# Re-timing of batch 2's value sums, batch 7's attention and the middle weights' conversion

## The chip, the cores and the metric

The kernel runs on one core of one Trainium2 chip. The metric is device time in microseconds (us) of one execution. The engines are PE (TensorE: matmuls; PEld its weight loads), DVE (VectorE), ACT (ScalarE), POOL (GpSimd) and SP (SyncE, which here only issues DMAs). Each takes its instructions strictly in the order in which they stand in its own stream; semaphores hold an instruction until what it reads or overwrites is ready.

## The reference

Eight batches (0 to 7) go through three layers. The first is attention with pooled keys and values (576 queries, keys and values averaged over groups of 8 to 72, 8 heads of 64); the second ("moe") turns its output `x` into `x*cos(theta)` and `x*sin(theta)`, mixes over tokens with two 576x576 weights and then over channels with `w_ch`; the third ("moe2") is two two-layer perceptrons.

```python
k_p = k.reshape(B, H, Sp, 8, D).mean(axis=3); v_p = ...        # Sp = 72
scores = scale * q @ k_p^T;  scores -= max
attn = exp(scores);  attn /= sum + 1e-9;  x = attn @ v_p
theta = x @ w_theta
zr, zi = x * cos(theta), x * sin(theta)
u = x + w_tok_r @ zr + w_tok_i @ zi
x = u + relu(u @ w_ch)
h = relu(x^T @ w_tok1) @ w_tok2;  u = x + h^T
out = u + relu(u @ w_ch1) @ w_ch2
```

## The kernel before

**Values in two parts.** Most products are made in a 32-bit form that keeps fewer bits than fp32, so an operand is split into a high and a low part (`Xh`/`Xl`, `vbh`/`vbl`, the two halves of `Z`), and each product is three matmuls. The weights arrive as 64-bit numbers; a *conversion* of one piece (`cq_step`, L251 to L278) makes it fp32 with operations on its two 32-bit words and then splits it (high part on ACT L302, low part on POOL or DVE L304). In its mode 2 the first operation, which drops the sign, is a bitwise AND on DVE (L257); in mode 1 it is an Abs on ACT (L231).

**A batch.** It has scores for four pairs of heads (`emit_sc`: `x<-bdk,q` on PE, maximum L547 and subtraction L548 on DVE, exponential L553 on ACT), the normalisation (`emit_norm`: sum L560, reciprocal L564 on DVE, scaling of `e` L565 and two small copies into `pl` L570 on POOL), transposes of the attention weights on PE (`emit_pt`, four of `e` and one of `pl`, L181), attention times values (`emit_av`: `x<-pt,vbh`, `x<-pt,vbl`, `x<-t,vlh`), theta in column groups of two token halves (`emit_theta`: `t<-wth`; cosine and sine L735 to L748, whose last two ACT operations, L741 and L742, use another activation table than the exponential), and `Z` (`emit_z`: product L766 on DVE, high part L780 on ACT, low part L781 on POOL). `x` below also names the PSUM banks through which scores, transposes of `R` and `x` for L766 go; a bank is free for the next user when the DVE operation that reads it is done.

**Token mixing.** For each of 8 output tiles (j, th) of a batch 27 matmuls `m<-wtk,Z` (24) and `m<-wtk,zt` (3) are added up in PSUM, 256 or 320 columns wide, and DVE adds the sum to `R` (L819, and L2273 for batch 0), after which `R` is stored (`scr_u`, SP).

**Key and value sums.** DVE sums groups of 8: `prep_k` (L406, from `kr`), `prep_v` (L416 from `vr`, and after a copy on ACT the low part L423 from the one buffer `sums`), `prep_vl` (L438 from `vlr`). `vr` has one buffer, so that the second half of a batch's values is loaded when the first has been summed.

**What sets the order.** Batch 0, and the attention and part of theta and Z of batch 1, are ordered by a planner (`first_batches`, L1777 to L2280). After it `issue_after(behind)` puts the first loads and sums for batch 2 behind all that it planned. For batches 1 to 7 `interleave` puts the 72 mixing steps of batch b (3 matmuls each) in order and *side steps* among them: attention and half of theta of batch b+1, loads and sums of batch b+2. A side step is issued at a due time of the table `P` in us of matmul work since the start of the batch. The framework then reorders each engine's stream by what it holds ready, so an instruction can end up well ahead of the place where it is issued. The middle weights (`w_ch`, `w_tok1`, `w_tok2`; 15 pieces of DVE work and more for the tails) are converted in batch 7 by `begin` and 19 `cq_step`s; they are used from 510 us on. The third layer follows from there and is not touched.

Of the kernel before, what the change touches and what calls it, by code (L numbers as in the profile page):

```python
# [19 lines left out]
P = {  # L20
    "lo": 0.24,
    "sc": (6.25, 8.41, 12.28, 13.41),
    "norm": 3.97,
    "pt": (22.02, 23.22, 25.71, 29.04, 30.75),
    "av": (26.38, 27.79, 31.91, 31.99),
    "th1": (0, 3.17),
    "z1": (5.39, 9.51),
    "th0": (36.38, 36.77, 37.89),
# [14 lines left out]
    "f_prep": (0.93, 4.0, 10.52, 8.07),  # L43
    "f_ws": (5.53, 0),
    "pl": (2, 2, 0, 0),
    "l_cq": (1.26, 1.0),
    "l_u": (11.67, 22.91, 4.84),
    "l_th1": (3.39, 3.6),
    "l_z1": (3.91, 8.29),
    "l_n": (0.0, 4.89, 2.84),  # L50
    "a_n": (2.91,),
    "a_cq": (1, 3, 5, 7),
    "a_th": (0,),
    "a_tr": 4,
    "md": (1.7, 2.0),
    "mo": 1,
}
F64_FLOOR = 2.0 ** -15
# [14 lines left out]
def tile_attn_moe(  # L73
# [20 lines left out]
    B = qT.shape[0]  # L94
# [26 lines left out]
    def later(dt, fn, *tags):  # L121
        dseq[0] += 1
        heapq.heappush(dq, (clk[0] + dt, dseq[0], fn, tags))
        tick()

    def flush():
        while dq:
            run_one()

    def st(tag, shape, dt, name=None):  # L130
        need(tag)
        return sb.tile(shape, dt, tag=tag, name=name or tag)
# [258 lines left out]
    def load_v(b, g):  # L391
        t = st("vr", [128, 2, 512], F32)
        nc.sync.dma_start(out=t, in_=vm[b, 2 * g:2 * g + 2].rearrange("g p t -> p g t"))
        vr_t[b, g] = t

    def load_vl(b):
        t = [st(x, [128, 512], F32, "vlr") for x in ("vlr", "n2")]
        for g in range(2):
            for r in range(3):
                nc.sync.dma_start(out=t[g][32 * r:32 * r + 32], in_=vl[b, 32 * g:32 * g + 32])  # L400
        vlr_t[b] = t
# [11 lines left out]
    def prep_v(b, g):  # L413
        vr = vr_t.pop((b, g))
        vs = st("sums", [128, 2, 64], F32)
        nc.vector.tensor_reduce(  # L416
            out=vs, in_=vr.rearrange("p g (d o) -> p g d o", o=8), axis=AX.X, op=ALU.add
        )

        def fin():  # L420
            for e in range(2):
                pr = slice(64 * e, 64 * e + 64)
                nc.vector.tensor_sub(  # L423
                    out=vlo["b"][pr, 2 * g:2 * g + 2, pr], in0=vs[pr],
                    in1=vbh[pr, 2 * g:2 * g + 2, pr].bitcast(F32),
                )

        for e in range(2):
            pr = slice(64 * e, 64 * e + 64)
            nc.scalar.copy(out=vbh[pr, 2 * g:2 * g + 2, pr], in_=vs[pr])  # L430
        later(1.0, fin, "sums", "vbl")

    def prep_vl(b):
        vr = vlr_t.pop(b)
        vs = st("vls", [128, 2, 64], F32)
        vh = st("vlsh", [128, 2, 64], F32R)
        for g in range(2):
            nc.vector.tensor_reduce(  # L438
                out=vs[0:96, g], in_=vr[g][0:96].rearrange("p (d o) -> p d o", o=8), axis=AX.X, op=ALU.add
            )  # L440
        nc.scalar.copy(out=vh[0:96], in_=vs[0:96])
        nc.gpsimd.tensor_sub(out=vh[32:64], in0=vs[32:64], in1=vh[32:64].bitcast(F32))
        m4 = mask[0:96, 0:4].unsqueeze(2)
        for g in range(2):
            nc.gpsimd.tensor_tensor(
                out=vlt[0:96, 2 * g:2 * g + 2].rearrange("p a e d -> p (a e) d"),
                in0=m4.to_broadcast([96, 4, 64]),
                in1=vh[0:96, g].bitcast(F32).unsqueeze(1).to_broadcast([96, 4, 64]),
                op=ALU.mult,
            )  # L450
# [1871 lines left out]
    def side_next(b):  # L2322
        n = b + 1
        s = []
        f = "f_" if b == 0 else ""
        for p in range(4):
            s.append((P[f + "sc"][p], lambda p=p: emit_sc(n, p)))
            s.append((P[f + "sc"][p] + P[f + "norm"], lambda p=p: emit_norm(n, p)))
        for p, t in zip((0, 1, 4, 2, 3), P[f + "pt"]):
            s.append((t, lambda p=p: emit_pt(n, p)))  # L2330
        for j, t in enumerate(P[f + "av"]):
            for th in range(2):
                s.append((t + 0.6 * th, lambda j=j, th=th: emit_av(n, j, th)))
        for g, t0, t1, lo in zip((2, 0, 1), P[f + "th0"], P[f + "z0"], (nc.gpsimd,) * 3):
            s.append((t0, lambda g=g: emit_theta(n, 0, g)))
            s.append((t1, lambda g=g, lo=lo: emit_z(n, 0, g, lo)))
        return s
# [12 lines left out]
    if True:  # L2350
        behind = first_batches()
        with ExitStack() as s:
            for i in behind:
                s.enter_context(tc.issue_after(i))
            if B > 2:
                load_v(2, 0)
                load_vl(2)
                prep_v(2, 0)
                load_v(2, 1)
                prep_v(2, 1)  # L2360
                prep_vl(2)
            flush()
        for b in range(1, B):
            last = b == B - 1
            side = []
            f = "l_" if last else "f_" if b == 0 else ""
            for g, a, z, lo in zip((0, 1), P[f + "th1"], P[f + "z1"], (nc.gpsimd,) * 2):
                side.append((a, lambda g=g: emit_theta(b, 1, g)))
                side.append((z, lambda g=g, lo=lo: emit_z(b, 1, g, lo)))
            if not last:  # L2370
                side += side_next(b)
            if b + 2 < B:
                side += side_load(b + 2)
            if last:
                def begin():
                    zt = st(f"zt{(b + 1) % 2}", [128, CV, 2], U32, "late0")
                    vs = [st(x, [128, 256, 2], U32, f"late_{x}") for x in ("vbh", "vbl", "vlh", "vll")]
                    vr = st("vr", [128, 3, CV], F32, "late1")
                    n = [int(x + 0.5) for x in P["l_n"]]
                    cq_use((["stg0", "stg1", "bdk"] + ([zt] + vs)[0:n[0]]),  # L2380
                           (["cvt0", "vlr"] + [vr[:, i] for i in range(3)])[0:1 + n[1]])
                    lo_m[0] = max(2, n[2])
                    cq_mode[0] = min(2, int(P["md"][0] + 0.5))
                    add_wch()
                    add_tok1()
                    add_tok2()
                    cq_load()
                side.append((0.0, begin))
                for i in range(19):
                    side.append((P["l_cq"][0] + P["l_cq"][1] * i, cq_step))  # L2390
                side.append((P["l_u"][0], lambda: load_u(0)))
                for j in range(4):
                    side.append((P["l_u"][1] + P["l_u"][2] * j, lambda j=j: split_u(0, j)))
            interleave(mix_steps(b), side)
        flush()
        cq_step(20)
        wq[:] = weight_steps(0, 256, (W_TAGS[0:4], W_TAGS[4:6], W_TAGS[6:8], W_TAGS[8:13]), (0,) * 6)
        wstep(2)

        def ch(b):  # L2400
            order = [(j, th) for j in range(4) for th in range(2)]
            if b in P["a_th"]:
                order = [(j, th) for th in range(2) for j in range(4)]
            for i, (j, th) in enumerate(order):
                emit_ch(b, j, th)
                if b == 0 and P["a_tr"] == i:
                    emit_tr(0, 0)
                    emit_tr(0, 1)
                if i % 2 == 0:
                    wstep()  # L2410

        if B > 1:
            load_u(1)
        ch(0)
        if B > 1:
            for j in range(4):
                split_u(1, j)
        for c in range(2 if P["a_tr"] < 8 else 0, 5):
            emit_tr(0, c)
        for b in range(B):  # L2420
            if b + 2 < B:
                load_u(b + 2)
            for f in range(2):
                emit_tok1(b, f)
            if b + 1 < B:
                ch(b + 1)
            for j in range(4):
                for th in range(2):
                    emit_tok2(b, j, th)
                    if th == 0 and j % 2 == 0:  # L2430
                        wstep()
                    if j == 1 and th == 0 and b + 1 < B:
                        for c in range(5):
                            emit_tr(b + 1, c)
                if b + 2 < B:
                    split_u(b + 2, j)
        wstep(1000)
        flush()
        channel_mix()
# [62 lines left out]
```

## Time and profile before

| what | value |
|---|---|
| three runs | 1274.97, 1275.24, 1278.01 us, median 1275.24 |
| profiled execution, span | 1275.0 us |
| mean granted TensorE clock | 0.993 |
| PE busy | 1248.5 us, 98% |
| DVE, ACT, POOL busy | 953.2, 656.4, 302.7 us |
| PE idle longest in the part that the change touches | 2.06, 0.95, 1.63, 2.99 us |

The profile is of one execution, and its own time is its span of 1275.0 us. Times below count from the start of the span. The mixing of batch 1 begins at 121.8 us, that of batch 6 at 409.5, that of batch 7 a little before 470, and `w_ch` at 510.4. A row of a timeline gives start, duration, engine, line, operation, output <- inputs, shapes and count; in square brackets stand the idle time before it and what ended it. Rows of one kind are merged and may overlap the next by some 0.2 us, so work is measured from start to start.

### The profile page before, as it was taken

Reading aid. Unit: us, or ns where it says so; the run is one execution under the profiler, and the core shown is the slowest. Engines: PE = TensorE matmul, PEld = TensorE weight load, DVE = VectorE, ACT = ScalarE, POOL = GpSimd, SP = SyncE. Lnnn points to the kernel's source line nnn. Section 1 sums busy time; section 2 is a strip of 40 time slices with the busy share of each in tenths; the row PEclk is TensorE's granted clock in tenths of the full one; section 3 lists DMA queues with packets and bytes.
Section 4 is the critical chain, followed back from the end, with each engine's and each line's share of the span. In section 5 each row is a group of like instructions: output and inputs, shape, how many; then the busy total and the mean of one; then the engine's idle time right before and its main releaser. Section 6 shows DMA issues by size and latency. Waiting matters only on the chain.

```text
span 1275.0 us, 22259 instructions
## 1 busy us (share of the span) xinstructions
PE 1248.5 (98%) x8132; PEld 1205.9 (95%) x8132; DVE 953.2 (75%) x1739; ACT 656.4 (51%) x1264; POOL 302.7 (24%) x301
## 2 busy tenths in 40 slices
PE   8999999999999989999999999999999999999998
PEld 5789999999999989899999999999999899999998
DVE  7995868586675993867775689986644598988894
ACT  4856566656756663334422256665554445444442
POOL 1382424334242441211110022320000032213122
PEclk9999999999999999999999999999999999999999
DMA  9523433232221132666782488984448966546621
GB/s 337 157 79 103 141 96 112 71 112 72 94 87 36 45 99 88 212 211 237 260 292 75 157 287 277 299 279 155 139 146 293 369 217 203 183 139 215 204 88 63
DMA packets 122126, 214.50 MB, mean 168 GB/s; under 512 B 11744, under 2 KB 68576, under 8 KB 122016
## 3 DMA queue, kind: packets, MB, share of 16 engines
q1 hardware_dynamic: 122016, 213.08, 50.4%
q8 instruction: 64, 1.05, 0.3%
q14 instruction: 46, 0.38, 0.1%
HBM read 134.39 MB, written 78.64 MB: 167 GB/s over the span
## 4 chain that ended last, share of the span: by engine, by line
PE 76%; DVE 11%; DMA 7%; ACT 2%; issue 2%; SPq 1%; POOL 0%; DVEq 0%; ACTq 0%; POOLq 0%
PE m L167 28%; PE x L167 26%; PE t L167 19%; PE x L181 3%; DMA ws<-w_ch 1%; DMA early<-w_tok 1%; DMA scr_x<-u 1%; DMA early<-w_theta 1%; DMA scr_w<-wo 1%; DMA k<-kT 1%; DMA q<-qT 0%; DMA vr<-vm 0%; DMA scr_g<-g 0%; DVE early L1713 0%; DMA stg<-w_ch 0%
## 5 line engine op out<-in xcount | busy, mean ns | idle before, releaser
L167 PE MATMUL m<-wtk,Z 128*128 128x256 f32 (+1 forms) x1536 | 259.6, 304 | 5.7 <-ACT Z L780 3.0
L167 PEld LDWEIGHTS m<-wtk,Z 128*128 128x128 f32 x1536 | 222.9, 192 | 8.1 <-ACT Z L780 3.2
L167 PE MATMUL x<-ope_Z,wa 128*128 128x384 f32 x492 | 94.8, 336 | 0.0
L167 PEld LDWEIGHTS x<-ope_Z,wa 128*128 128x128 f32 x492 | 86.3, 188 | 0.1
L1412 POOL TENSOR_TENSOR o<-o,u 128x384 f32<-128x384 f32 x12 | 16.3, 1380 | 285.4 <-DVE u L1400 217.8
L781 POOL TENSOR_TENSOR Z<-tmp,Z 128x1024 fp32r<-128x1024 f32 x26 | 62.9, 2419 | 86.7 <-ACT Z L780 86.7
L1046 POOL TENSOR_TENSOR wsum<-wm 128x128 f32<-128x128 f32 (+1 forms) x18 | 13.6, 755 | 269.9 <-DVE wm L1036 262.5
L167 PE MATMUL t<-wth,Xh 128*128 128x256 f32 x432 | 59.6, 279 | 0.0
L167 PE MATMUL m<-wtk,zt 128*128 128x256 f32 (+1 forms) x192 | 57.4, 299 | 0.0
L167 PEld LDWEIGHTS t<-wth,Xh 128*128 128x128 f32 x432 | 55.2, 188 | 0.7 <-DVE tmp L717 0.2
L766 DVE TENSOR_TENSOR tmp<-x,tmp 128x1024 f32<-128x1024 f32 x26 | 31.7, 1220 | 28.9 <-ACT tmp L742 15.5
L167 PE MATMUL t<-ope_Z,wa 128*128 128x384 f32 x234 | 48.1, 336 | 1.3 <-ACT p L1320 1.3
L167 PE MATMUL m<-ope_Z,wa 128*128 128x384 f32 x234 | 48.1, 336 | 0.0
L167 PE MATMUL x<-ope_R,wa 128*128 128x384 f32 x228 | 45.6, 346 | 0.9 <-DVE p L1325 0.9
L167 PE MATMUL x<-bdk,q 128*128 128x144 f32 x298 | 42.9, 293 | 2.7 <-DVE tmp L766 2.1
L167 PEld LDWEIGHTS x<-bdk,q 128*128 128x128 f32 x298 | 39.4, 194 | 4.2 <-DVE tmp L766 2.3
L167 PE MATMUL m<-ope_Xl,wa 128*128 128x384 f32 x204 | 42.6, 336 | 0.6 <-ACT ope_Xl L1159 0.6
L167 PEld LDWEIGHTS x<-ope_R,wa 128*128 128x128 f32 x228 | 41.6, 194 | 1.5 <-DVE p L1325 1.5
L167 PEld LDWEIGHTS t<-ope_Z,wa 128*128 128x128 f32 x234 | 41.3, 188 | 1.6 <-ACT p L1320 1.6
L167 PE MATMUL t<-ope_Xl,wa 128*128 128x384 f32 x204 | 42.5, 336 | 0.0
L167 PE MATMUL x<-ope_Xh,wa 128*128 128x384 f32 x192 | 39.4, 336 | 2.5 <-DVE p L1325 1.3
L167 PEld LDWEIGHTS m<-ope_Z,wa 128*128 128x128 f32 x234 | 41.5, 188 | 0.0
(476 smaller groups left out, 3487.5 us busy)
## 6 DMA issues: line engine op xcount, KB each, us to landing
wa<-scr_w SPq DMA_DIRECT2D x42, 512.0 KB, 5.4
scr_g<-g SPq DMA_DIRECT2D x108, 192.0 KB, 2.9
scr_w<-wo SPq DMA_DIRECT2D x42, 256.0 KB, 3.3
scr_u<-R SPq DMA_DIRECT2D x32, 288.0 KB, 2.1
u<-scr_u SPq DMA_DIRECT2D x32, 288.0 KB, 4.1
scr_w<-wo SPq DMA_DIRECT2D x18, 512.0 KB, 3.3
scr_x<-u SPq DMA_DIRECT2D x32, 288.0 KB, 2.1
raw_n<-scr_x SPq DMA_DIRECT2D x24, 384.0 KB, 4.3
```

The costliest lines, as they stand in the source:

```text
L167: nc.tensor.matmul(out=o, lhsT=l, rhs=r, start=start, stop=stop, skip_group_check=skip)
L181: nc.tensor.transpose(o, i, ident)
L766: nc.vector.tensor_tensor(out=tmp, in0=px.unsqueeze(1).to_broadcast([128, 2, 512]), in1=tmp, op=ALU.mult)
L781: later(1.0 if lo is nc.vector else 0.0, lambda: lo.tensor_sub(out=zl, in0=zv, in1=zh.bitcast(F32)), tg, zg)
L1046: nc.gpsimd.tensor_tensor(out=s[:, 2], in0=a11, in1=a21, op=ALU.subtract)
L1412: nc.gpsimd.tensor_tensor(out=u22[d].t, in0=u22[d].t, in1=u2[d].t, op=ALU.add)
```

## The change

Three things are re-timed; no arithmetic of the result is taken away.

1. The sums of batch 2's values (`prep_v`, `prep_vl`) leave the block behind the planner and become side steps of batch 1, due at 3.0, 10.0 and 12.5 us.
2. The side steps of batch 7 (issued in batch 6) get due times of their own: transposes 6 us earlier, theta 1 to 5 us earlier, Z 4 us earlier.
3. `begin` and nine of the 19 `cq_step`s are issued in batch 6, from 27.2 us on, the other ten in batch 7, 2.1 us apart; and the mode is 1 instead of 2 (`"md"`, rounded).

```diff
+    "j_v": (3.0, 10.0, 12.5),
...
+    "g_pt": (16.0, 17.2, 19.7, 22.5, 23.8),
...
-    "md": (1.7, 2.0),
+    "md": (1, 2.0),
...
-        f = "f_" if b == 0 else ""
+        f = "f_" if b == 0 else "g_" if n == B - 1 else ""
...
                 load_v(2, 0)
                 load_vl(2)
-                prep_v(2, 0)
-                load_v(2, 1)
-                prep_v(2, 1)
-                prep_vl(2)
             flush()
...
-            if last:
+            if b == 1 and B > 2:
+                side += [(P["j_v"][0], lambda: (prep_v(2, 0), load_v(2, 1))),
+                         (P["j_v"][1], lambda: prep_vl(2)), (P["j_v"][2], lambda: prep_v(2, 1))]
+            if b == B - 2:
                 def begin():
...
-                side.append((0.0, begin))
-                for i in range(19):
+                t, dt, n = P["g_cq"]
+                side.append((P["g_begin"], begin))
+                for i in range(n):
+                    side.append((t + dt * i, cq_step))
+            if last:
+                for i in range(19 - P["g_cq"][2]):
                     side.append((P["l_cq"][0] + P["l_cq"][1] * i, cq_step))
```

Line numbers of the changed kernel are 9 higher from L60 on (L416 is L425 there).

**DVE, end of the planned part.** Before, from the update of `R` by the sixth tile of batch 0 (`m_1259`) on:

```order
L2273 TENSOR_TENSOR R_398<-m_1259,R_398 128x320
L2143 SCALAR_TENSOR_TENSOR tmp_1287<-tmp_1287 64x512
L2187 TENSOR_TENSOR tmp_1287<-x_1250,tmp_1287 128x512
L2273 TENSOR_TENSOR R_398<-m_1297,R_398 128x320
L416 TENSOR_REDUCE sums<-vr 128x128
L438 TENSOR_REDUCE vls<-vlr 96x64
L423 TENSOR_TENSOR vbl<-sums,vbh 64x2x64 x2
L438 TENSOR_REDUCE vls<-vlr 96x64
L748 SCALAR_TENSOR_TENSOR tmp_1395<-tmp_1395,t_1370 128x512
L416 TENSOR_REDUCE sums<-vr 128x128
L423 TENSOR_TENSOR vbl<-sums,vbh 64x2x64 x2
L766 TENSOR_TENSOR tmp_1395<-x_1435,tmp_1395 128x1024
```

In the changed kernel, the rows from the last key sum of the planner on, which reach up to the same update of `R` by `m_1259`:

```order
L1786 TENSOR_REDUCE sums<-kr 128x144
L2134 SCALAR_TENSOR_TENSOR tmp_1186<-tmp_1186,t_1155 128x512
L425 TENSOR_REDUCE sums<-vr 128x128
L2134 SCALAR_TENSOR_TENSOR tmp_1232<-tmp_1232,x_1188 128x512
L2189 TENSOR_TENSOR tmp_1186<-x_1143,tmp_1186 128x1024
L432 TENSOR_TENSOR vbl<-sums,vbh 64x2x64 x2
L425 TENSOR_REDUCE sums<-vr 128x128
L2282 TENSOR_TENSOR R_398<-m_1107,R_398 128x256
L2189 TENSOR_TENSOR tmp_1232<-x_1238,tmp_1232 128x1024
L432 TENSOR_TENSOR vbl<-sums,vbh 64x2x64 x2
L415 TENSOR_REDUCE sums<-kr 128x144
```

Both value sums now stand in front of two of batch 0's updates of `R` and of batch 1's last Z products, where before they stood behind all of these and in front of L766 of batch 1; the sums of `vlr` stand earlier still. On SP the load that the second sum reads now follows a load of `kr` directly, where before two stores `scr_u` stood in between.

**ACT, exponentials of batch 7 (in batch 6).** Before, from the first cosine step of theta's half-done group to the last exponential (`wch`: high parts of conversions):

```order
L740 ACTIVATE tmp_4878<-tmp_4878 128x512
L741 ACTIVATE tmp_4878<-tmp_4878 128x512
L742 ACTIVATE tmp_4878<-tmp_4878,phase 128x512
L302 ACTIVATE wch_5489<-cvt_5480 128x256
L553 ACT_TABLE_LOAD
L553 ACTIVATE e<-e 128x5x144
L302 ACTIVATE wch_5489<-vlr 128x256
L780 CAST Z_4814<-tmp_4878 128x2x512
L553 ACTIVATE e<-e 128x5x144
L302 ACTIVATE wch_5528<-late_5460 128x256
L553 ACTIVATE e<-e 128x5x144 x2
```

In the changed kernel, from the high part of the group before to the last exponential (one exponential stands ahead of these rows):

```order
L789 CAST Z_4814<-tmp_4840 128x2x512
L562 ACTIVATE e<-e 128x5x144
L749 ACTIVATE tmp_4893<-tmp_4893 128x512
L750 ACT_TABLE_LOAD
L750 ACTIVATE tmp_4893<-tmp_4893 128x512
L751 ACTIVATE tmp_4893<-tmp_4893,phase 128x512
L562 ACT_TABLE_LOAD
L562 ACTIVATE e<-e 128x5x144
L789 CAST Z_4814<-tmp_4893 128x2x512
L562 ACTIVATE e<-e 128x5x144
```

The exponentials were one run behind one table load; now the sine steps of theta stand between the second and the third, with a table load on each side.

**POOL, the same place.** Before, from the last low part of Z to the last copy into `pl`:

```order
L781 TENSOR_TENSOR Z_4814<-tmp_4878,Z_4814 128x2x512
L565 TENSOR_TENSOR e<-e,sm_4939 128x5x144
L304 TENSOR_TENSOR wch_5528<-late_5460,wch_5528 128x256
L570 COPY pl<-e 128x5x2x8 x2
L565 TENSOR_TENSOR e<-e,sm_4979 128x5x144
L570 COPY pl<-e 128x5x2x8 x2
L565 TENSOR_TENSOR e<-e,sm_5012 128x5x144
L570 COPY pl<-e 128x5x2x8 x2
L565 TENSOR_TENSOR e<-e,sm_5031 128x5x144
L570 COPY pl<-e 128x5x2x8 x2
```

In the changed kernel:

```order
L790 TENSOR_TENSOR Z_4814<-tmp_4840,Z_4814 128x2x512
L574 TENSOR_TENSOR e<-e,sm_4916 128x5x144
L579 COPY pl<-e 128x5x2x8 x2
L574 TENSOR_TENSOR e<-e,sm_4924 128x5x144
L579 COPY pl<-e 128x5x2x8 x2
L790 TENSOR_TENSOR Z_4814<-tmp_4893,Z_4814 128x2x512
L574 TENSOR_TENSOR e<-e,sm_4972 128x5x144
L574 TENSOR_TENSOR e<-e,sm_4992 128x5x144
L579 COPY pl<-e 128x5x2x8 x4
```

Batch 6's last low part of Z moved from before all four scalings to between the second and the third. On PE the transposes of `pl` stand behind 75 mixing matmuls of batch 6, where they stood behind 114; the 39 between are 12 of 256 columns and 27 of 320.

## Rows read from the trace of the kernel before

**Rows 1.** The page, first section: busy time by engine.
```profile
PE 1248.5 (98%) x8132; PEld 1205.9 (95%) x8132; DVE 953.2 (75%) x1739; ACT 656.4 (51%) x1264; POOL 302.7 (24%) x301
```

**Rows 2.** Waits of PE in 100:200 and 409:510 (total, times, longest).
```profile
PE x L167 <- DVE tmp L766: 2.1, 1, 2.1
...
PE m L167 <- ACT Z L780: 3.0, 1, 3.0
PE m L167 <- DVE R L819: 1.6, 1, 1.6
PE x L167 <- DVE t L607: 0.9, 1, 0.9
```

**Rows 3.** Windows: length, busy PE, PEld, DVE, ACT, POOL, clock, DMA, GB/s.
```profile
134.06:137.47 3.41, 3.41 (x17) 3.09 (x16) 3.41 (x8) 3.36 (x5) 2.38 (x1) 0.50 0.51 102
...
438.60:463.30 24.70, 23.75 (x178) 22.56 (x177) 23.79 (x65) 18.19 (x45) 7.53 (x7) 1.00 0.32 92
...
472.00:478.80 6.80, 5.97 (x27) 5.97 (x28) 6.63 (x16) 1.86 (x5) 3.83 (x3) 0.50 0.52 163
```

**Rows 4.** Timeline of PE, end of batch 0's mixing and batch 1.
```profile
117.85 1.33 PE L167 MATMUL m<-wtk,Z 128*128 128x320 f32 x8
...
133.62 1.42 PE L167 MATMUL x<-bdk,q 128*128 128x144 f32 x6 [2.06 <-DVE tmp L766]
...
138.03 1.05 PE L167 MATMUL m<-wtk,Z 128*128 128x320 f32 x6
```

**Rows 5.** Timeline of PE, batches 6 and 7.
```profile
418.57 1.39 PE L167 MATMUL x<-bdk,q 128*128 128x144 f32 x10
419.80 0.60 PE L181 MATMUL x<-con,R 128*128 128x128 f32 x4
...
420.60 1.11 PE L167 MATMUL m<-wtk,Z 128*128 128x256 f32 x8
...
421.66 1.04 PE L167 MATMUL m<-wtk,Z 128*128 128x320 f32 x6
...
437.01 0.71 PE L181 MATMUL x<-con,pl 128*128 128x128 f32 x5
...
472.83 1.65 PE L167 MATMUL m<-wtk,Z 128*128 128x256 f32 x6 [2.99 <-ACT Z L780]
...
479.43 1.07 PE L167 MATMUL t<-wth,Xh 128*128 128x256 f32 x8
```

**Rows 6.** Timeline of DVE, end of the planned part and batch 1.
```profile
112.08 0.69 DVE L2125 SCALAR_TENSOR_TENSOR tmp<-tmp,x 128x512 f32<-128x512 f32 x1 [3.37 <-ACT tmp L2122]
...
114.10 0.42 DVE L2273 TENSOR_TENSOR R<-m,R 128x256 f32<-128x256 f32 x1 [0.20 <-PE m L167]
...
130.12 1.22 DVE L416 TENSOR_REDUCE sums<-vr 128x128 f32<-128x1024 f32 x1 [3.00 <-DMA vr<-vm]
...
132.34 1.22 DVE L766 TENSOR_TENSOR tmp<-x,tmp 128x1024 f32<-128x1024 f32 x1
```

**Rows 7.** Chain of waits, the second load of values.
```profile
124.74 5.29 DMA vr<-vm
```

**Rows 8.** Timeline of ACT, exponentials of batch 7.
```profile
421.00 1.28 ACT L553 ACT_TABLE_LOAD   x1
422.30 0.80 ACT L553 ACTIVATE e<-e 128x720 f32<-128x720 f32 x1
...
427.16 0.81 ACT L553 ACTIVATE e<-e 128x720 f32<-128x720 f32 x1 [1.56 <-DVE e L548]
```

**Rows 9.** Timeline of POOL, scalings and copies of batch 7.
```profile
424.42 2.39 POOL L781 TENSOR_TENSOR Z<-tmp,Z 128x1024 fp32r<-128x1024 f32 x1 [0.20 <-ACT Z L780]
...
433.17 1.43 POOL L565 TENSOR_TENSOR e<-e,sm 128x720 f32<-128x720 f32 x1
434.67 0.52 POOL L570 COPY pl<-e 128x80 f32<-128x80 f32 x2
```

**Rows 10.** Timeline of DVE, batch 6: a sum of exponentials.
```profile
423.13 0.90 DVE L560 TENSOR_REDUCE ss<-e 128x10 f32<-128x720 f32 x1
```

More of the change, by code (lines that the diff above doesn't have):

```diff
@@ L45 @@
     "pl": (2, 2, 0, 0),
[L46 to L49, printed above, removed]
+    "j_v": (3.0, 10.0, 12.5),
+    "g_sc": (3.0, 5.0, 8.5, 9.6),
+    "g_norm": 3.5,
+    "g_pt": (16.0, 17.2, 19.7, 22.5, 23.8),
+    "g_av": (20.4, 21.8, 25.2, 25.4),
+    "g_th0": (31.2, 33.5, 37.0),
+    "g_z0": (34.0, 37.6, 41.0),
+    "g_begin": 27.2,
+    "g_cq": (29.0, 2.2, 9),
+    "l_cq": (1.5, 2.1),
+    "l_u": (3.0, 13.0, 4.0),
+    "l_th1": (0.0, 2.9),
+    "l_z1": (5.4, 8.6),
     "l_n": (0.0, 4.89, 2.84),
```

## The prediction

> **What bounds the kernel now.** I read the page first: PE is busy for 98% of the span [rows 1], so only its idle time, and the time that it runs at a lower clock, can be won. The list of PE's waits comes next, for the stretches that the change touches: one wait of 2.1 us in batch 1, and three of 3.0, 1.6 and 0.9 us at the turn from batch 6 to batch 7 [rows 2]. In between no wait of PE on another engine is listed, and the third layer is not touched. The windows then show what these waits do to the clock: behind the 2.06 us PE runs at 0.50 of the clock, which is the 1.2 GHz level, for 3.41 us, and behind the 2.99 us for some 6.8 us, while over 438.6 to 463.3, with 0.95 us of idle time, it stays at 1.00 [rows 3]. The timelines of PE and DVE, last, say what each wait was for.
>
> In batch 1, PE's scores wait for a bank that L766 reads. L766 starts at 132.34, because in DVE's order a value sum L416 stands in front of it, and that waited 3.00 us for its DMA and ended at 131.3 [rows 6]; the load had been issued at 124.74 and took 5.29 us [rows 7]. At the turn of batches DVE is the late one: over 438.6 to 463.3 it is busy for 23.79 of 24.70 us, with conversions among its work for the batch [rows 3], and R and Z come late by that.
>
> **The change part by part.** The sum is made against the profiled execution, 1275.0 us, which is 0.24 below the median of the three runs.
>
> *Value sums of batch 2.* The wait removed is 2.06 us. The stretch behind it, from 133.62 to 138.03, took 4.41 us [rows 4]; it holds 6 score products, 4 transposes and the mixing up to the first 320-column product. Batch 6 makes 10 score products from 418.57 to 419.80 and the rest from there to 421.66 [rows 5], so the same work at full clock is 0.6 x 1.23 + 1.86 = 2.60. The clock cost 1.81. Together that is -3.9.
>
> The new place is the end of the planned part. DVE was idle there for 3.37 us up to 112.08 [rows 6], in which the first L416 (1.22 us) fits. The second needs `vr`, whose only buffer is free when the first has been summed, at about 110; with 5.29 us for the load it starts at 115.3 and ends at 116.5. Behind it on DVE stands the update of `R` which before ran at 114.10 [rows 6]; it now ends at 117.0. Behind that wait L766's counterpart for batch 1's Z, and PE, which needs the bank of that update back at 117.85, when it starts the next tile [rows 4]. The margin is 0.9 us. The loads of `vlr` and `kr` that are issued around it may take it away. I bound it by nothing and 1.5 us of waiting and take 0.5. The `vlr` sums and the key sum of batch 3 go further up among the planned work, where DVE waits for others too; I count them at nothing, and allow 0.6 either way, half of the 1.22 us of a value sum.
>
> *Turn of batches 6 and 7.* Waits of 0.95, 1.63 and 2.99 sum to 5.6 [rows 2]. From 472.83 to 479.43 PE did 25 products of 256 columns and 6 of 320 in 6.60 us [rows 5]. A group of 8 at full clock takes 1.11 (256 columns) [rows 5] or 1.33 (320) [rows 4], less the 0.16 by which a row overlaps the next (418.57 + 1.39 against 419.80 [rows 5]); that is 0.118 and 0.146 each, and 3.8 for all. The clock cost 2.8. If all goes, that is -8.3. I take it whole: theta and Z of batch 7 are issued 1 to 5 us earlier; the conversions, issued 2.1 us apart, stand behind them on DVE; and the ANDs move from DVE to ACT, whose share over 438.6 to 463.3 is 18.19 of 24.70 [rows 3] and thus has room. What is late next if DVE keeps its backlog is the same R update and Z, at most the 8.3 again.
>
> *New waits inside batch 6.* ACT's order now has the sine steps between the second and the third exponential, with two more table loads of 1.28 us [rows 8]. I put the second exponential at about 422.0, near the first of before, since its pair's subtraction stands behind a sum that needs the first exponential and behind L766. Behind it come three steps of theta (512 columns each, so 0.80 x 512/720 = 0.57) and two loads: 422.0 + 0.8 + 1.7 + 2.6 = 427.1 for the third, where it is now (427.16) [rows 8]. But L780 of Z follows it (1024 columns, 1.1 us by the same measure), and then on POOL the low part of Z (2.39), two scalings of 1.4 and four copies (0.52 for two) [rows 9]: 427.1 + 0.7 + 1.1 + 2.4 + 2.7 + 0.9 = 434.9, each a little under its row for the overlap. Before, the last copies were done at 434.67 + 0.52 = 435.2 [rows 9], and PE took the transposes of `pl` at 437.01 [rows 5], unhindered. Now 12 products of 256 and 27 of 320 columns fewer stand in front of them, 1.4 + 3.9 = 5.35 us, so PE is there at 431.7, or 432.5 with the small waits below. It waits 2.4 us; queued behind it on PE are the products of attention and values, and behind these DVE's L607 and theta of batch 7. A wait of 2.06 us cost 1.8 us of clock above, one of 0.95 none; 2.4 is nearer to the former: +1.8. The bounds are 0 (PE's other delays cover it, or the exponentials are early) and 5.2 + 2.8 (as the 2.99 us wait did).
>
> The small waits: sums of exponentials (0.90 each [rows 10]) now wait on DVE for exponentials that come one by one, and in front of them the scores' subtraction and an update of `R` are held. I take 0.3 for the former, 0.4 for the latter, and 0.3 for banks of the transposes taken earlier: +1.0, between 0 and 2.
>
> The sum: 1275.0 - 3.9 + 0.5 - 8.3 + 2.4 + 1.8 + 1.0 = 1268.5.
>
> **A rule that speaks against it.** In rows 8 the load takes 1.28 us, and the exponential starts 1.30 us after the load did. The Trainium skill, "ScalarE: Activation LUTs", section "What ACT_TABLE_LOAD costs", gives about the same load and adds a drain of some 1.38 us to every switch. By that rule two more switches would cost 2.8 us more than I counted, on ACT in front of the third exponential. No such gap shows between load and exponential here; the drain could only lie ahead of the load.
>
> **The rivals.**
> (a) *The waits go and none comes.* For it: PE is the bound, and POOL's last copies ended 1.8 us before PE asked. Against it: POOL's order. 1275.0 - 3.9 - 8.3 = 1262.8, up to 1264.5 with the first small waits.
> (b) *A switch of tables costs more than its load.* If ACT loses 1.4 us more at each of the two new switches, the copies end at 437.7 and PE waits 5.2: 1268.5 + 2.8 = 1271.3. Against it speaks the 1.30 us between load and exponential.
> (c) *The gain is given back.* DVE stays behind at the turn, since the conversions begin in batch 6 as they already did; only their ANDs are gone. Half of the 8.3 stays, and the new `pl` wait comes on top: 1268.5 + 4.2 = 1272.7, and with all of it 1276.8. For it: DVE is at 96% there [rows 3], and the number of conversions is the same.
> (d) *Slower: a value sum blocks DVE in front of `R`.* If the second load of values lands late (as late as it did, at 124.74 + 5.29 = 130.0 [rows 7]), the update of `R` behind it ends at 131.7 and PE stands from 117.85 on, 13.8 us, and 1.8 of clock: 1268.5 - 0.5 + 15.6 = 1283.6. Against it: the load is no longer issued behind the stores of `R`. It decides from a landing at about 124 on (1268.0 + 6 to 7 of waiting, some 2 of clock and a slipped Z of batch 1 give 1279).
> (e) *The change doesn't move what it says.* The sums float elsewhere by the framework's order, or the waits in batch 6 only change names: 1275, within (c).
>
> **How the numbers follow.** A measurement of this kernel can tell 0.3%, or 3.8 us, from no change: faster is below 1271.4, slower above 1279.0. My forecast, 1265.5 to 1271.4, has 0.50; (a) 0.17; (b) 0.06, half of it on either side of 1271.4; (c) and (e) 0.19; (d) 0.08. Faster is then 0.50 + 0.17 + 0.03 = 0.70, the same 0.03 + 0.19 = 0.22, slower 0.08. The range runs from 1263.5, which leaves out some of (a), to 1274.0, which leaves out (d) and the end of (c).
>
> **What the changed profile would show.** Right: in PE's waits for 100 to 200 us no L766 line, at most 1.5 us on an update of `R` near 118; the value sums on DVE near 109 and 115; three table loads on ACT between 416 and 428 where there was one; a wait of PE of 2 to 3 us on the copies of `pl` at about 432, a lower clock behind it, and none between 438 and 480. Wrong: the list of waits still has Z or `R` at the turn (c), no `pl` line (a), one of 5 us (b), or one of over 6 us near 118 (d); or a new wait at the start of `w_ch`, if the conversions spread over batch 7 come too late for it, which I counted at nothing because it begins 31 us after batch 7's theta at 479.43 [rows 5].

## The result and the profile after

The changed kernel is slower: 1282.16 us median of five runs (1281.57 to 1282.57) against 1275.24 of the kernel before. The ratio is 1.0054, 95% interval 1.004 to 1.0068. The forecast was 1268.5, with a range of 1263.5 to 1274.0.

The profiled execution has a span of 1280.6 us against 1275.0, and its own time was 1282.35: some 1.75 us lie around the span. Where each stage gained or lost follows from the first instruction of batch 1 (121.78 before, 127.19 after), of batch 6 (409.46, 411.03) and of the `w_ch` stage (510.37, 514.86).

| stretch | before | after | difference | forecast |
|---|---|---|---|---|
| start to batch 1 | 121.78 | 127.19 | +5.41 | +0.5 |
| batch 1 to batch 6 | 287.68 | 283.84 | -3.84 | -3.9 |
| batch 6 to `w_ch` | 100.91 | 103.83 | +2.92 | -3.1 |
| `w_ch` to the end | 764.63 | 765.74 | +1.1 | 0 |

The gain in batch 1 came as worked out. The loss lies in two places: in the planned part ahead of batch 1, which the prediction put at nothing, and at the turn of batches 6 and 7. The last 1.1 us lie in the third layer, in single waits that differ by 0.2 to 0.7; this stretch took 764.2 in e10 and 766.4 in e6 (below), which change nothing in it, so that 1.1 is within what executions differ by.

First the page, the line that answers to [rows 1]; PE's busy time is the same, so idle time was added:

```profile
PE 1248.2 (97%) x8130; PEld 1205.7 (94%) x8132; DVE 951.7 (74%) x1720; ACT 664.3 (52%) x1285; POOL 301.3 (24%) x301
```

PE's waits after, in 60 to 125 us and in 409 to 520; these answer to [rows 2]. From 125 to 409 none is listed, so the L766 wait has gone:

```profile
PE x L176 <- DVE t L1999: 3.8, 1, 3.8
PE x L176 <- DVE tmp L2189: 1.5, 1, 1.5
...
PE m L176 <- DVE R L828: 4.7, 2, 4.2
PE x L190 <- POOL pl L579: 2.7, 1, 2.7
```

In the kernel before, the first two were 0.9 (L1990) and 0.4 (L2180). The windows behind three of the waits after (columns as in [rows 3]):

```profile
99.30:102.70 3.40, 3.37 (x16) 3.40 (x17) 1.93 (x4) 1.48 (x4) 0.00 (x0) 0.59 0.49 137
437.50:441.10 3.60, 3.60 (x19) 3.60 (x19) 2.39 (x6) 2.55 (x9) 0.00 (x0) 0.55 0.00 0
473.16:479.70 6.54, 6.54 (x27) 6.54 (x28) 6.16 (x19) 2.57 (x7) 1.96 (x3) 0.57 0.54 165
```

The mean clock is near the half level (1.2 GHz) in each, and (1 - clock) x length gives 1.4, 1.6 and 2.8 us.

**The planned part.** ACT's timeline after; the first row is the Abs of the first piece of `w_ch`:

```profile
70.37 0.44 ACT L240 ACTIVATE cvt<-stg 128x256 f32<-128x256 f32 x1 [3.22 <-POOL wtk L1750]
...
74.59 1.28 ACT L1863 ACT_TABLE_LOAD   x1
```

The conversions of batches 6 and 7 had always reached up into batch 0: their first piece is ready as soon as its staging buffer is. In mode 2 its first step is on DVE; in mode 1 it is this Abs on ACT, which needs a conversion buffer that POOL still reads. It stands 3.22 us, and behind it the table load of batch 1's exponentials, which the kernel before had at 71.19:

```profile
71.19 1.28 ACT L1854 ACT_TABLE_LOAD   x1
```

DVE's L2189 is late by that, and PE by 1.16 us (80.51 against 79.35).

DVE's timeline after, up to the operation that PE waits 3.8 us for:

```profile
88.17 1.22 DVE L270 TENSOR_SCALAR cvt<-cvt 128x256 f32<-128x256 f32 x1
...
89.86 0.67 DVE L447 TENSOR_REDUCE vls<-vlr 96x64 f32<-96x512 f32 x1
...
92.01 0.42 DVE L1989 TENSOR_TENSOR pt<-x,pt 128x256 fp32r<-128x256 f32 x1 [0.69 <-ACT pt L1987]
92.98 0.68 DVE L447 TENSOR_REDUCE vls<-vlr 96x64 f32<-96x512 f32 x1 [0.55 <-POOL vlsh L451]
93.58 1.31 DVE L273 TENSOR_SCALAR cvt<-cvt 128x256 uint32<-128x256 uint32 x1
94.92 1.45 DVE L279 SCALAR_TENSOR_TENSOR cvt<-stg,cvt 128x256 uint32<-128x256 uint32 x1
96.40 1.37 DVE L285 SCALAR_TENSOR_TENSOR cvt<-stg,cvt 128x256 uint32<-128x256 uint32 x1
97.69 0.48 DVE L2282 TENSOR_TENSOR R<-m,R 128x320 f32<-128x320 f32 x1
98.20 1.86 DVE L1999 TENSOR_TENSOR t<-x,t 32x320 fp32r<-32x320 f32 x4
```

L1999 follows, 3.99 us later than L1990 did (94.21); 1.16 of this is the delay from above. What is new in the other 2.8 us are the two sums of `vlr` (L447; 1.2 us from start to start) and the idle time in which DVE now waits for ACT (0.69) and POOL (0.55). The conversion steps L270, L273, L279 and L285 take 1.2 to 1.45 us each, where 0.3 to 0.4 is usual, but most of that is not new. In the kernel before they stood beside POOL's work too:

```profile
88.67 1.21 DVE L261 TENSOR_SCALAR cvt<-cvt 128x256 f32<-128x256 f32 x1
...
90.61 1.09 DVE L264 TENSOR_SCALAR cvt<-cvt 128x256 uint32<-128x256 uint32 x1
...
92.39 1.39 DVE L276 SCALAR_TENSOR_TENSOR cvt<-stg,cvt 128x256 uint32<-128x256 uint32 x1
```

There the piece's five steps took 4.9 us from start to start, against 5.3 for the four of now. So 2.4 of the 2.8 us come from the sums and the waits at their place, and 0.4 from the conversion steps.

**The turn.** DVE and POOL after, around PE's wait of 4.2 us, which ends with the last row's R:

```profile
466.97 2.52 DVE L279 SCALAR_TENSOR_TENSOR vlr<-bdk,vlr 128x256 uint32<-128x256 uint32 x1
469.41 0.81 DVE L270 TENSOR_SCALAR late<-late 128x256 f32<-128x256 f32 x1
470.14 2.56 DVE L285 SCALAR_TENSOR_TENSOR vlr<-bdk,vlr 128x256 uint32<-128x256 uint32 x1
472.62 0.48 DVE L828 TENSOR_TENSOR R<-m,R 128x320 f32<-128x320 f32 x1
```

```profile
466.81 2.40 POOL L790 TENSOR_TENSOR Z<-tmp,Z 128x1024 fp32r<-128x1024 f32 x1 [4.15 <-ACT Z L789]
...
470.03 2.38 POOL L790 TENSOR_TENSOR Z<-tmp,Z 128x1024 fp32r<-128x1024 f32 x1
```

Two steps of 0.41 us begin 0.1 to 0.2 us after a low part of Z on POOL and end 0.3 us after it. R stands behind them. The kernel before paid the same toll: its L257, 0.25 us elsewhere, lasted 2.46 under a low part of Z:

```profile
466.16 2.46 DVE L257 TENSOR_SCALAR cvt<-stg 128x192 uint32<-128x192 uint32 x1
```

```profile
465.96 2.54 POOL L781 TENSOR_TENSOR Z<-tmp,Z 128x1024 fp32r<-128x1024 f32 x1 [1.15 <-ACT Z L780]
```

**The `pl` wait** came as forecast, 2.70 against 2.4. ACT's order gives the reason as worked out, with POOL's last copies at 435.77 to 436.66; here is the switch of tables between the exponentials:

```profile
424.31 0.61 ACT L749 ACTIVATE tmp<-tmp 128x512 f32<-128x512 f32 x1
424.94 1.28 ACT L750 ACT_TABLE_LOAD   x1
426.24 0.63 ACT L750 ACTIVATE tmp<-tmp 128x512 f32<-128x512 f32 x1
```

Neither ahead of the load nor behind it is there a gap of over 0.03 us. A switch cost its 1.28 us.

### The profile page after: what moved, and what is told of

Read it like the earlier page. It is cut to its first block, busy times and chain, and to the rows that moved or that the text cites. A ratio compares the mean times of both kernels' runs of the same rounds, so it can differ in the third digit from the quotient of the medians.

```text
span 1280.6 us, 22271 instructions
## 1 busy us (share of the span) xinstructions
PE 1248.2 (97%) x8130; PEld 1205.7 (94%) x8132; DVE 951.7 (74%) x1720; ACT 664.3 (52%) x1285; POOL 301.3 (24%) x301
## 4 chain that ended last, share of the span: by engine, by line
PE 79%; DVE 8%; DMA 5%; ACT 4%; issue 2%; POOL 2%; SPq 1%; POOLq 0%; DVEq 0%; ACTq 0%
PE m L176 29%; PE x L176 27%; PE t L176 20%; PE x L190 3%; DMA ws<-w_ch 1%; DMA scr_x<-u 1%; DMA early<-w_theta 1%; POOL wtk L1750 1%; DMA k<-kT 1%; DVE raw_n L1172 1%; SPq L1595 0%; DMA early_w<-w_tok 0%; DVE p L1330 0%; DMA stg<-w_ch 0%; DVE early L1722 0%
```

## The experiments

All times are medians, with the ratio to the kernel before in the same comparison (1275.2 to 1275.7 us).

| run | median | ratio, 95% interval |
|---|---|---|
| changed kernel | 1282.16 | 1.0054, 1.004 to 1.0068 |
| e1 mode 2 | 1280.82 | 1.005, 1.0031 to 1.0068 |
| e2 `vlr` sums behind | 1279.71 | 1.0045, 1.0032 to 1.0058 |
| e3 low parts of Z on DVE | 1276.92 | 1.0016, 1.0008 to 1.0025 |
| e4 no shift of batch 7 | 1276.62 | 1.002, 1.0009 to 1.003 |
| e5 value sums alone | 1277.48 | 1.0015, 0.9999 to 1.0031 |
| e6 second sum alone | 1272.04 | 0.9971, 0.9956 to 0.9985 |
| e7 e6 + split + low parts on DVE | 1266.16 | 0.9925, 0.9904 to 0.9945 |
| e8 e7 with the shift | 1271.09 | 0.9958, 0.9945 to 0.9971 |
| e9 Abs alone | 1276.83 | 1.001, 0.9998 to 1.0022 |
| e10 low parts on DVE alone | 1270.91 | 0.9963, 0.9948 to 0.9978 |
| e11 e7, low parts on POOL | 1271.98 | 0.997, 0.9958 to 0.9981 |
| e12 second sum + low parts | 1266.81 | 0.9924, 0.9906 to 0.9941 |

**e1, the changed kernel in mode 2.**

```diff
-    "md": (1, 2.0),
+    "md": (2, 2.0),
```

> The changed kernel with the sign dropped on DVE again (mode 2), all else as changed. Theory: the Abs on ACT that stands in the planned part waits there for a conversion buffer that POOL still reads (3.2 us) and holds the exponentials behind it; so the table load ahead of them goes from 74.6 back to about 71.2, PE's wait on L2189 from 1.5 to 0.4, and batch 1 starts 1.2 us earlier or a little less, since the AND (1.0 us) comes back to DVE in front of L1999. At the turn of batches 6 and 7 the ANDs come back to DVE too, and R's wait (4.2) grows or stays. Total: the changed kernel's 1282.2 less 1.2, plus 0 to 2. Rival: the value sums alone delay the planned part; then the exponentials may move but PE's wait on L2189 stays at 1.5, and the time with it.

On ACT the table load is back, on PE the first wait falls as forecast and the second doesn't:

```profile
71.26 1.28 ACT L1863 ACT_TABLE_LOAD   x1
```

```profile
78.41 3.70 PE L176 MATMUL x<-nat_v,pool 128*128 128x512 f32 x8 [0.51 <-DVE tmp L2189]
97.25 0.38 PE L176 MATMUL x<-pt,vbh 128*128 128x320 f32 x1 [3.91 <-DVE t L1999]
```

Batch 1 starts at 125.11, 2.1 us earlier and more than the 1.2 expected. The wait gives 1.0 of this; the other 1.1 lies ahead of it, where the changed kernel's clock was 0.54 between 69 and 72 us and that of e1 was not lowered. R's long wait at the turn was expected to grow and fell to 2.19 (another of 1.60 came in batch 7): one step (L273, 2.50 us) was held ahead of R instead of two. Which steps fall under POOL's operation is a matter of where the stream stands at that moment. The time, 1280.82, is 0.2 below the expected range; its runs spread from 1277.1 to 1284.9, so that it says little by itself.

**e2, the `vlr` sums behind the planned part again.**

```diff
                 load_v(2, 0)
                 load_vl(2)
+                prep_vl(2)
...
-                         (P["j_v"][1], lambda: prep_vl(2)), (P["j_v"][2], ...
+                         (P["j_v"][2], lambda: prep_v(2, 1))]
```

> The changed kernel with the sums of vlr of batch 2 put back behind the planned part; the sums of vr stay side steps of batch 1. Theory: on DVE the two sums of vlr (0.67 each) and a wait of 0.55 for POOL's vlsh stand in front of the conversion and of L1999; without them L1999's wait falls from 3.8 to about 1 to 1.5, the lower clock behind it (1.4 us) goes too, and batch 1 starts at about 123 to 124 instead of 127.2. PE's wait on L775 in batch 1 stays away. Total 1282.2 - 3.5 = 1278.7 (1277.5 to 1280). Rival: the conversion and the late exponentials hold L1999, not these sums; then its wait stays above 3 and the time within 1 us.

```profile
95.85 0.39 PE L176 MATMUL x<-pt,vbh 128*128 128x320 f32 x1 [0.71 <-DVE t L1999]
123.68 1.21 PE L176 MATMUL t<-wth,Xh 128*128 128x256 f32 x8 [1.26 <-DVE tmp L2145]
```

The wait on L1999 falls from 3.84 to 0.71, so the `vlr` sums made it; the conversion steps ahead of it still take 1.2 to 1.5 us each. Batch 1 starts at 123.68, and the clock stayed up between 84 and 130. A wait of 1.26 that nobody had expected comes in its place: the second low part of the `vr` sums (L432, 3.96 us for two where 0.59 is usual) is done only when POOL's low part of Z is (POOL at 116.5 to 121.4), and theta's tail stands behind it. 1279.71 against 1278.7 expected; the rival is out.

**e3, batch 7's low parts of Z on DVE.**

```diff
-        for g, t0, t1, lo in zip((2, 0, 1), P[f + "th0"], P[f + "z0"], (nc.gpsimd,) * 3):
+        for g, t0, t1, lo in zip((2, 0, 1), P[f + "th0"], P[f + "z0"], ((nc.vector if n == B - 1 else nc.gpsimd),) * 3):
```

> The changed kernel with the three low parts of Z that are made for batch 7's first half in batch 6 on DVE instead of POOL. Theory: DVE's conversion steps L279 and L285 (0.41 us alone) last 2.5 us each because POOL's low part of Z (2.4 us) runs at that time, and R's update stands behind them; without POOL's operation they last 0.4, R is added about 4 us earlier less the 1.2 that a low part takes on DVE, PE's wait of 4.2 falls to 0 to 2 and the half clock behind it (2.7) goes: 1276 to 1279. The pl wait falls as well, by up to 2.4, as POOL is free for the scalings: then 1273 to 1277. Rival: DVE is late by the amount of its own work; then with 3.6 us more of it R comes later, the wait grows to 5 or more, and the time is 1282 to 1286.

PE's waits in 409 to 520, and DVE's rows for the same steps as above:

```profile
PE x L190 <- POOL pl L579: 2.7, 1, 2.7
PE m L176 <- DVE R L828: 1.0, 3, 0.4
```

```profile
467.12 0.42 DVE L279 SCALAR_TENSOR_TENSOR vlr<-bdk,vlr 128x256 uint32<-128x256 uint32 x1
467.45 1.22 DVE L775 TENSOR_TENSOR tmp<-x,tmp 128x1024 f32<-128x1024 f32 x1
468.59 0.48 DVE L828 TENSOR_TENSOR R<-m,R 128x320 f32<-128x320 f32 x1
468.99 0.42 DVE L285 SCALAR_TENSOR_TENSOR vlr<-bdk,vlr 128x256 uint32<-128x256 uint32 x1
...
469.79 1.22 DVE L790 TENSOR_TENSOR Z<-tmp,Z 128x1024 fp32r<-128x1024 f32 x1
```

DVE has more work and R comes 4 us earlier: 1276.92, 5.2 us less. The steps take 0.42 again. This decides against the rival, by which DVE is late by the amount of its own work. A low part is also done sooner on DVE (1.22 us for 2.4), but the wait that fell is one on R, which doesn't need it. A part of the expectation failed: the `pl` wait is unchanged. The low part that stands between the scalings on POOL is that of batch 6's second half, which this edit leaves where it was.

**e4, batch 7 at its old due times.**

```diff
-        f = "f_" if b == 0 else "g_" if n == B - 1 else ""
+        f = "f_" if b == 0 else ""
```

> The changed kernel with batch 7's attention and theta at their old due times; begin, the conversions and the value sums stay as changed. Theory: the wait on the pl copies (2.7, and 1.7 of clock behind it) goes, since 39 mixing products stand in front of those transposes again; but Z of batch 7 and R are late again as in the kernel before (waits of 1.6 and 3.0, 2.8 of clock). So the turn costs about what it did before, 8.3, instead of 11.8: 1282.2 - 3.5 = 1278.7, within 2. Rival: the conversions' due times are what makes R wait; then the 4.2 us wait stays as it is and only the pl wait goes: 1277.5.

1276.62: 2.1 us better than the theory, just outside its margin of 2, and nearer to the rival's 1277.5; the waits decide between them. The `pl` wait is gone, and so is the 4.2 us wait on R (0.31 is left); Z comes late by 1.58, L616 by 1.16, and batch 7 gets two waits on R (0.79, 1.52). The clock stayed at its full level at the turn. The rival, that the conversions' due times make R wait, is out. The change also gave new due times to theta, Z and the loads of `u` inside batch 7 (`l_th1`, `l_z1`, `l_u`), which its description leaves out; this run keeps them, and no run has them alone.

**e5, the value sums alone, on the kernel before** (the `j_v` steps of the change and nothing else of it).

> The kernel before with the move of batch 2's value sums alone; mode 2, batch 7 and the conversions as before. Theory: the sums of vlr in the planned part hold DVE (two of 0.67 and a wait of 0.5 for POOL) and push the conversion under POOL's work, so PE's wait on L1990 grows from 0.9 to 3.5 to 4, with 1.4 us of lower clock behind it; PE's wait on L766 in batch 1 (2.06 and 1.8 of clock) goes. Batch 1 starts 4 to 4.5 us later, and its length falls by 3.8: no change in all, 1275.2 + 0.4 (within 1.5). Rival: without the Abs on ACT the sums find idle time of DVE, the wait on L1990 stays near 1, and the kernel gains the 3.9 forecast: 1271.5.

```profile
PE x L167 <- DVE t L1990: 3.9, 1, 3.9
PE t L167 <- DVE tmp L2136: 1.3, 1, 1.3
PE x L167 <- DVE tmp L2180: 0.5, 1, 0.5
```

The wait on L1990 is there without the Abs, and there is none on L766. The wait on L2180 stays at 0.5, so its 1.5 in the changed kernel is not due to the sums. The 1.3 on L2136 is e2's new wait again: the second low part of the `vr` sums (L423, 3.79 us for two) lies under POOL's low part of Z. Batch 1 starts 5.3 us later (127.08), more than the 4 to 4.5 expected, and its stretch up to batch 6 is 4.0 shorter. 1277.48, 1.9 us more than before (interval -0.1 to +4.0 us): the gain of 3.9 is given back, at least nearly in full.

**e6, one sum moved, on the kernel before.** `prep_v(2, 1)` leaves the block behind the planner and is held behind the last DVE instruction issued by 7 us of batch 1:

```diff
                 load_v(2, 1)
-                prep_v(2, 1)
                 prep_vl(2)
...
+            if b == 1 and B > 2:
+                def second_sum():
+                    i = [x for x in nc.cur_bb.bb.instructions if "DVE" in str(x.engine)][-1]
+                    with tc.issue_after(i):
+                        prep_v(2, 1)
+                side.append((7.0, second_sum))
```

> The kernel before with one instruction moved: the second sum of batch 2's vr, which waits for its DMA, is put behind L766 of batch 1 on DVE; all other sums stay behind the planned part, and the turn is as before. Theory: L766 no longer waits for that DMA and starts near 129 instead of 132.34, PE's wait of 2.06 and the half clock behind it go, and nothing of the planned part moves: 1275.2 - 3.9 = 1271.3 (1271 to 1272.5). Rival: the low part of the first sum (L423) or ACT's steps are as late, so that L766 starts after 131 and a wait of about 1 stays: 1274.

```profile
127.92 1.23 DVE L766 TENSOR_TENSOR tmp<-x,tmp 128x1024 f32<-128x1024 f32 x1 [1.97 <-ACT tmp L742]
...
131.78 1.21 DVE L416 TENSOR_REDUCE sums<-vr 128x128 f32<-128x1024 f32 x1
```

L766 runs 4.4 us earlier than in [rows 6] (3.4 counted from the start of batch 1, which is at 120.72), the sum finds its place behind it, and PE has no wait in 100 to 200 us. 1272.04 us, 3.6 less: the whole gain of the change's first part, without its cost.

**e7 and e8, the parts that pay, without and with the shift of batch 7.** Both are the changed kernel with e6's move for the sums, mode 2 and e3's edit; e7 has e4's edit too.

> The changed kernel with the second vr sum as the only one moved (behind L766 of batch 1), the sign dropped on DVE (mode 2), batch 7's attention and theta at their old due times, and the low parts of Z of batch 7's first half on DVE; begin and the conversions are issued as in the changed kernel. Theory: batch 1 starts at 121.8 again and has no wait (-3.9 against the kernel before); at the turn no conversion step lasts 2.5 us under these low parts, R waits under 0.5, Z of batch 7 is the last to come (up to 1.6, as with the old due times in the changed kernel), and the clock stays up: 4 to 6 of the 8.3 are won. Total 1275.2 - 3.9 - 5 = 1266 (1264.5 to 1269). Rival: DVE has 3.6 us more of low parts and the ANDs again, R or Z come late by 2 to 3 us and the clock falls: 1270 to 1272.

> As the run before it, but with batch 7's attention and theta at the changed kernel's due times. Theory: the wait of 2.7 on the pl copies and 1.7 of clock behind it are back, since POOL's order puts batch 6's own Z between the scalings; Z and R of batch 7 are early, with waits under 0.5. Total 1275.2 - 3.9 - 8.3 + 4.4 + 0.5 = 1268 (1266.5 to 1270), 0 to 2 above the run without the shift. Rival: early theta saves more than the pl wait costs (Z and R of batch 7 keep DVE's backlog from PE in batch 7 too): 1265 or less, and below the run without the shift.

e7 took 1266.16, as forecast; R's wait at the turn (1.3) is longer than the 0.5 that the theory gave it. e8 took 1271.09, 4.9 more: the `pl` wait (2.7) is back and, in batch 7, one of 1.4 on R. It is 1.1 above the range that the theory gave. The shift of batch 7 costs here more than it saves, but not by all of the 4.9. In the two profiled executions the stretch from batch 6 to `w_ch` is 2.1 us longer with it (96.68 against 94.59); another 3.3 lie ahead of batch 1, where the edits are the same and e8's clock was at 0.50 to 0.85 between 60 and 75 us.

**e9, the Abs alone, on the kernel before** (`"md": (1, 2.0)`).

> The kernel before with the sign dropped on ACT (mode 1) alone. Theory: on ACT the Abs of the first converted piece stands in the planned part, waits about 3.2 us for the conversion buffer and holds the table load of the exponentials to 74.6; PE's wait on L2180 grows from 0.4 to 1.5 and batch 1 starts 1.0 to 1.2 us later; on DVE one AND (1.0) less stands in front of L1990, which does not come later than that. At the turn the ANDs leave DVE, and R and Z come up to 1.5 us earlier. Total 1275.2 + 1.1 - 1 = 1275 (1273.5 to 1276.5). Rival: the Abs costs nothing without the value sums beside it; then PE's wait on L2180 stays at 0.4 and the time falls to 1273.

```profile
70.23 0.44 ACT L231 ACTIVATE cvt<-stg 128x256 f32<-128x256 f32 x1 [3.21 <-POOL wtk L1741]
...
74.45 1.28 ACT L1854 ACT_TABLE_LOAD   x1
```

The same 3.2 us, and PE's wait on L2180 is 1.42. With e5's 0.5 this shows that the wait needs the Abs and nothing else of the change. 1276.83, 0.3 above the expected range; the interval holds no change. At the turn R's first wait fell to 0.32 and Z's rose to 4.05, so that the ANDs' leaving DVE bought nothing.

**e10 and e11, the low parts of Z by themselves.** e10 is the kernel before with e3's edit alone; e11 is e7 without it.

> The kernel before with the three low parts of Z of batch 7's first half on DVE instead of POOL, alone. Theory: the kernel before pays the same thing at its turn: one AND (L257) of 2.46 us under POOL's low part stood in front of L766 and of Z (PE's wait of 2.99). Without it the Z wait falls below 1 and the clock behind it stays up; the first R wait (1.63), which follows L766 and a step of 1.33, falls less. 1275.2 - 2.5 to - 5 = 1270 to 1272.7. Rival: with DVE busy all the time, 3.6 us more work on it brings the waits back: 1275 to 1277.

> The fastest kernel so far (second vr sum behind L766, mode 2, conversions issued from batch 6 on, old due times for batch 7) with the low parts of Z of batch 7's first half back on POOL. Theory: conversion steps under them last up to 2.5 us again, and R's or Z's wait of 2 to 3 us at the turn comes back: 1266.2 + 2.5 to + 5 = 1268.7 to 1271. Rival: the spread of the conversions over two batches is what freed the turn; then it stays at 1266 to 1267.

PE's waits in e10 in 409 to 520 us:

```profile
PE m L167 <- DVE R L819: 1.5, 2, 1.3
...
PE x L167 <- DVE t L607: 0.9, 1, 0.9
```

The Z wait of 3.0 us [rows 2] is gone: 1270.91, 4.8 less. That wait was on the high part of Z (L780), which doesn't need the low parts. Over the same work as the 438.60:463.30 of [rows 3], which is 2.2 us earlier here, DVE is busy for the same 23.79 of 24.70 us:

```profile
436.40:461.10 24.70, 23.76 (x178) 22.57 (x177) 23.79 (x66) 18.22 (x45) 7.21 (x8) 1.00 0.30 92
```

So a share of 96% there did not make the wait.

e11 took 1271.98, 5.8 more than e7 and 1.0 above its expected range. A held step of 2.47 us is back (L266 at 461.07), but R's longest wait is 1.64, not the 2 to 3 expected; two more, of 1.10 and 1.53, came in batch 7. The time is the same as e6's (1272.04), which has the conversions as the kernel before. So the split of the conversions over two batches, together with the new due times inside batch 7, is worth nothing that these runs can tell.

**e12, the two edits that pay, on the kernel before** (e6's and e3's).

> The kernel before with two edits and nothing else of the change: the second vr sum behind L766 of batch 1, and the low parts of Z of batch 7's first half on DVE. Theory: the two gains are in different places and add: 3.6 (as measured for the sum alone) and 4.8 (for the low parts alone), 1275.6 - 8.4 = 1267 (1266 to 1268.5), the same as with the split of the conversions over two batches, which is then worth nothing. Rival: the split gives part of the gain; then 1269 or more.

1266.81 us: ratio 0.9924, interval 0.9906 to 0.9941. It is faster than the kernel before by 8.9 us and than the changed kernel by 15.4, with no wait of PE over 1.3 us between 60 and 520 us. e7's 1266.16 can't be told from it.

## Why the prediction was wrong

- **The value sums in batch 1, -3.9: right.** It came out at -3.84, and e6 gives 3.6 for this alone. The price at the R update near 118 was 0, inside its bounds: both sums stand in front of it, and PE has no wait there. In e2 and e5, though, the low part behind the second sum cost 1.3.
- **The planned part, nothing with 0.6 either way: the step that failed first.** The prediction said that the `vlr` sums "go further up among the planned work, where DVE waits for others too". They cost 2.9 us of waiting and 1.4 of clock (e2 and e5). DVE had no idle time where they went: in the kernel before, none of its rows from 72.36 to 94.21 shows any ahead of it. The sums' own 1.2 us thus went straight into L1999's delay, and with them 1.2 of idle time: one sum waits for POOL, and the conversion step that had run while DVE waited for ACT now stands behind it.
- **The AND that moves to ACT: missed.** The prediction looked for it between 438 and 463, where ACT has room. Its first piece stands 370 us earlier. The rows of ACT's order there would have shown an Abs on a buffer that POOL frees, ahead of a table load. It cost PE 1.16 us (1.0 in e1 and e9).
- **The turn, -8.3: the largest miss.** It came to -0.9: waits of 0.48 + 4.22 and 2.8 of clock against 5.57 and 2.8. The waits had been put down to DVE's share of 96% and to Z's due time. e10 removes the Z wait at the same share. What made the waits are single steps of 0.25 to 0.4 us behind that window, which show as 2.5 us busy while POOL works. So earlier due times only changed which step was caught, and R took the place of Z. Rival (c) named the wait, R at the turn, without this cause, and gave 1272.7 to 1276.8.
- **The `pl` wait, +2.4 and 1.8 of clock: right**, 2.70 and 1.6. e4 and e8 show that it comes with the shift.
- **The small waits, +1.0: none came.** PE's first wait of the stretch in the changed kernel is that for `pl`.
- **A dearer switch of tables, rival (b): wrong**, as the rows of the switch show.
- **Rival (d), slower:** the outcome was on this side, and DVE was late ahead of batch 1, but by the `vlr` sums and the Abs, and not by a DMA. The second load held DVE for 0.65 us and PE not at all.
- **The base.** The sum was made against a span of 1275.0 as if it were the time of that execution. With 1.75 us around the span, as in the changed kernel's, that execution took about 1276.8. This is an error of some 1.75 us in the direction of the result. With it, and with the +5.6 of the four stretches in place of -6.5, the difference between 1282.35 and 1268.5 is accounted for.

The Trainium skill, "SBUF — State Buffer", section "Who interferes with whom", states the rule that bears on the turn: a DVE instruction with two inputs in SBUF contends for a port pair with a GpSimd instruction that reads SBUF, as does one in a two-port mode with GpSimd, and the one that issues second blocks until the first has finished. The rows agree: L279 and L285 have two inputs in SBUF and last until POOL's operation ends (2.52 and 2.56 us against 0.42 in e3). L766 of the kernel before, with one of its two inputs in PSUM, took 1.21 us at 463.60 with POOL at work throughout (463.52 to 464.82), and 1.21 at 470.49 with POOL idle. L257 has one input and was held too; whether it ran in a two-port mode no row shows.

The one that waits can also be POOL. In the kernel before this low part of a conversion, 0.74 us elsewhere, took 2.79:

```profile
450.50 2.79 POOL L304 TENSOR_TENSOR wch<-vlr,wch 128x256 fp32r<-128x256 f32 x1 [2.19 <-ACT wch L302]
```

Seven steps of DVE beside it, from 450.66 on, took their usual 0.28 to 0.41 us each.

## What to carry to other kernels

A busy share is no proof that an engine is overloaded. Compare one instruction's duration in the stretch with its duration elsewhere, and where it is several times longer, look at what POOL does at that moment: moving three POOL operations to the busy DVE gave 4.8 us here, where the re-timing of batch 7 gave none. When a change takes an instruction from one engine to another, follow its first instance in the streams' order and not only the batch in which it is issued; and to remove one wait, move only the instruction that waits.

## What was not expected of the hardware

The same wait of PE did not always lower the clock. In e6 the Z wait of 2.99 us at the turn is the same as in the kernel before, where some 6.8 us at 0.50 followed [rows 3]; in e6 the clock stays up (window around that wait, columns as above):

```profile
457.00:475.00 18.00, 13.14 (x98) 12.38 (x97) 16.95 (x34) 6.90 (x13) 9.59 (x8) 1.00 0.41 134
```

In e8 the `pl` wait of 2.7 us left the clock at 1.00 as well, where the changed kernel fell to 0.55. So the clock terms of the prediction (1.8 and 2.8 us) are what one execution paid; other executions of the same waits paid nothing. The spread of single runs of one kernel follows this: of e6's twelve, the three with a mean clock of 1.000 took 1268.9 to 1269.9 us, the one with 0.993 took 1276.1.

The clock also fell where no edit lies. Between 69 and 72 us it was 0.53 in the kernel before and 0.54 in the changed one, and not lowered in e6 and e11; batch 1 starts at 121.78 in the kernel before, and at 120.72 and 120.60 in these two. So a stretch of two single executions can differ by a microsecond and more (3.3 us in e8) without an edit in it. What decides it stays open.
